# Softmax row sums of 16 heads in one matmul set, a fourth folding transfer, and seven tiles of weights in place of eight

## The chip, the cores and the metric

One core of a Trainium2 chip runs the whole program. The metric is the device time of one execution in microseconds (us). Three runs of the kernel before gave 1788.33, 1789.01 and 1789.20; the median, 1789.01, is what the changed kernel is held against.

The engines named below: PE multiplies matrices (PEld are its weight loads), ACT applies functions to elements, DVE adds and multiplies elements, POOL and SP here mostly issue DMA transfers. Each engine works through its own queue in order.

## The reference

The input is a sequence of 2048 tokens of width 1024. The output mixes two blocks with a gate per token. Block A is attention with 32 heads of width 32:

```
q, k, v = split(x @ wqkv)                      # 32 heads, width 32
scores  = q @ k.T * 32 ** -0.5
p       = softmax(scores, axis=-1)
a       = (p @ v, heads side by side) @ wo
```

Block B picks one of 64 experts for each of 32 heads per token (`peer` in the names) and sums their rows. The result is `g * a + (1 - g) * b` with `g = sigmoid((x * gate_w).sum(-1))`.

The change is in the softmax's denominators: for each head and each of the 2048 queries, the sum of `exp(score)` over all 2048 keys.

## The kernel before

The program first makes Q, K and V (Strassen-like products on PE), then runs the attention, and then multiplies by `wo`. Only the attention is touched.

Its loop runs over 512 **steps**. Step k = 16h + kt stands for key tile kt (128 keys) of head h (0 to 31). Two steps make a pair, and the order of work in a pair is written out by hand at the end of the loop: first the scores of the new pair, then the products with V of the pair before, then whatever the table `todo` holds for these steps, then the sums.

- `scores` (`L1402`) writes 128 keys x 2048 queries into four banks of `ring`, seven PSUM banks used in turn. ACT (`L1412`) takes `exp` of one, two or three banks at a time into a tile of weights: `P`, or `accd` for one key tile of each head. The cuts between these activations depend on which bank the pair begins with.
- `pv` (`L1423`) multiplies a tile of weights by V into `o`.
- `presum` adds the tiles of weights of one head to a tile of sums, `ACC[h]`. Most are added by DVE (`L1449` the first two, `L1451` the others). The key tiles in `SUMS[h]`, three or four, are kept off DVE: the first of them is written to `accd` straight away, and the others are added to it by accumulating transfers that POOL issues (`L1444`). `merge` (`L1454`) adds `accd` to `ACC[h]` on DVE, 5 steps into the next head.

**Tiles.** `P` has eight places, four in a pool on the right side of SBUF and four on the left. `p_places` gives each key tile the place that is due first, by a rule that takes a tile as read 5 steps after it was written, or 9 if a transfer reads it. An activation that writes into a place waits until its readers are through. `ACC[h]` has three tiles, taken in turn: `acc0`, `acc1` and `vhl`.

**From 128 rows to one sum.** After `merge`, `ACC[h]` holds 128 partial sums per query, one in each partition. Its upper half is added to its lower half by accumulating transfers that POOL issues: `fold_half` (`L1459`, 128 to 64 rows), `fold_quarter` (`L1462`, to 32) and, for heads 0 to 23, `fold_eighth` (`L1465`, to 16). `gather` (SP) copies the rows that are left into the tile `rb0`: eight heads of 16 rows fill its 128 partitions. Then `group_sums` (`L1435`) sums over the partitions of all these heads at once: four matmuls, one for each quarter of the queries, with a matrix of zeros and ones as weights (`sel8` for eight heads, `sel` for four). ACT copies the result to `ssb` (`L1484`), SP stores one row per head to DRAM (`smd`), `load_r` brings back the sums of four heads as 128 x 64 (`rr`), and `norm_r` (DVE `L1517`, `L1518`) makes the factors, which SP stores to `rd`.

The heads form the sets 0 to 7, 8 to 15, 16 to 23 (16 rows each) and 24 to 27 (32 rows each, without `fold_eighth`). Heads 28 to 30 go through `head_sums` with a matmul set of their own, and head 31 is done after the loop.

The due steps stand in the table `todo`. Counted from the first step of head h: `merge` 21, `fold_half` 25, `fold_quarter` 32, `fold_eighth` 39, `gather` 44, and for the last head of a set `group_sums` 52, then `load_r` 6 and `norm_r` 10 steps after that, each group of four heads 6 steps after the one before. They only set the place in each engine's queue; an instruction also waits for its data.

SP's queue in each head holds, in order: the store of the head before (`od<-osb`, key tile 0), five loads of K and Q for the next head (key tile 2), a quarter of V for the next four heads (key tile 7), a piece of `wo` (key tile 11, from head 8 on), and a `gather` (key tile 12).

Of the kernel before, what the change touches and what calls it, by code (L numbers as in the profile page):

```python
# [9 lines left out]
F32 = mybir.dt.float32  # L10
# [21 lines left out]
def gated_mha_peer_kernel(ctx, tc, xT, wqkv, wv, wo, wq, k12, ug, v, out):  # L32
# [8 lines left out]
    nc = tc.nc  # L41
# [24 lines left out]
    ident = const.tile([128, 128], F32, name="ident")  # L66
    ones = const.tile([128, 32], F32, name="ones")
# [5 lines left out]
    warm = const.tile([128, 112], F32, name="fill")  # L73
# [4 lines left out]
    def dma(dst, src, queue=nc.sync):  # L78
        a, b = (ap.bitcast(F32) if ap.dtype == F32R else ap for ap in (dst, src))
        return queue.dma_start(a, b)  # L80
# [588 lines left out]
    wl_, wh_, pools = [], [], []  # L669
# [588 lines left out]
    P, pools = {}, {}  # L1258
# [2 lines left out]

    def p_places():

        due, last, order = list(range(-8, 0)), [0] * 8, []
        for k in range(H * NT):
            h, kt = divmod(k, NT)
            if kt != SUMS[h][0]:
                i = min(range(8), key=lambda j: due[j])
                due[i], last[i] = k + (9 if kt in SUMS[h] else 5), k
                order.append(i)  # L1270
        by_last = sorted(range(8), key=lambda j: last[j])
        return iter([by_last.index(i) for i in order])

    def p_tile(h, kt):

        i = next(pools["places"])
        P[h, kt] = pools["left" if i >= 4 else "right"].tile([128, S], F32, name=f"P{i}")
        return P[h, kt]

    def first_scores(*banks):  # L1280
# [40 lines left out]
    ACC = {}  # L1321

    def new_acc(h):
        if h % 3 == 2 and h < H - 2:
            ACC[h] = keep.tile([128, S], F32, name="vhl")
        else:
            ACC[h] = wk.tile([128, S], F32, name=f"acc{h % 3 if h < H - 2 else h % 2}", bufs=1)

    def load_vhl(i):
        if i == 0:  # L1330
# [7 lines left out]
    wk = Pool("wk", bufs=2)  # L1338

    new_acc(0)  # L1340
    nc.vector.memset(sel, 0.0)
    for i in range(4):
        nc.vector.memset(sel[32 * i:32 * i + 32, i:i + 1], 1.0)
    sel8 = warm[:, :32]
    nc.vector.tensor_reduce(sel8[:, :8], ident.rearrange("p (j r) -> p j r", j=8), axis=AX.X, op=OP.max)
    nc.vector.memset(sel8[:, 8:], 0.0)
    vpool = Pool("vpool", bufs=2)
    kq = Pool("kq")
    pools["left"] = Pool("ppl")
# [79 lines left out]

    def rowsum(ps, *srcs, by=ones):
        for src in srcs:
            for qc in range(NQ):
                yield nc.tensor.matmul(ps[32 * qc:32 * qc + 32, :], by,  # L1435
                                       src[:, qc * 512:(qc + 1) * 512],
                                       start=(src is srcs[0]), stop=(src is srcs[-1]))

# [25 lines left out]
    def fold_eighth(h):  # L1464
        nc.gpsimd.dma_start(ACC[h][:16], ACC[h][16:32], accum_op=OP.add)  # L1465

    NE = 24

    def set_of(h):
        return (h // 8 * 8, 8) if h < NE else (NE, 4)  # L1470

    def gather(h):
        first, n = set_of(h)
        if h == first:
            F[first] = keep.tile([128, S], F32, name="rb0")
        rows, j = 128 // n, h - first
        dma(F[first][rows * j:rows * j + rows], ACC.pop(h)[:rows])

    def group_sums(first, n):
        i, = ring_banks(1)  # L1480
        for ins in rowsum(ring[:, i, :], F.pop(first), by=sel8 if n == 8 else sel):
            on_ring(ins, i)
        o = wk.tile([128, 512], F32, name="ssb")
        on_ring(nc.scalar.activation(o, ring[:, i, :], AF.Copy), i)  # L1484
# [80 lines left out]
    def at(step, f, *a):  # L1565
        todo.setdefault(step, []).append((f, a))

    for h in range(H):
        base = h * NT
        g, j = divmod(h, 4)  # L1570
        if h < H - 1:
            at(base + NT, finish, h)
            at(base + NT + 5, merge, h)
            if h >= NP:
                at(base + NT + 8, head_sums, h)
            else:
                at(base + NT + 9, fold_half, h)
                first, n = set_of(h)
                if n == 8:
                    at(base + 2 * NT, fold_quarter, h)  # L1580
                    at(base + 2 * NT + 7, fold_eighth, h)
                    at(base + 2 * NT + 12, gather, h)
                else:
                    at(base + 2 * NT + 4, fold_quarter, h)
                    at(base + 2 * NT + 8, gather, h)
                if h == first + n - 1:
                    step = base + (3 * NT + 4 if n == 8 else 2 * NT + 14)
                    at(step, group_sums, first, n)
                    for i in range(n // 4):
                        at(step + 6 + 6 * i, load_r, first // 4 + i)  # L1590
# [320 lines left out]
```

## Time and profile before

| what | us |
|---|---|
| three runs, median | 1789.01 (1788.33 to 1789.20) |
| the profiled execution | 1789.59 |
| its span in the trace | 1787.5 |
| PE busy (ends of matmuls modelled) | 1782.3 |
| DVE busy | 1513.2 |
| ACT busy | 1307.3 |
| POOL busy | 297.3 |

The shares change with the stage. In the page's 40 slices ACT is busy nine tenths or more in the 15th to the 36th, and one to six tenths everywhere else: that is the attention loop, from about 606 to 1611 us, and what matters here lies in it. The granted TensorE clock is full in all slices. The rows of the trace give the start in us from the span's start, the length, the engine, the line of the program, the operation, the tiles it writes and reads, and in brackets the idle time of the engine before it with what ended it ("issue" is time in which it waited for nothing that the profile shows). A group's row gives the count, the busy time, the mean of one in ns, and the idle time before them.

### The profile page before, as it was taken

The page shows a single profiled execution, that of the slowest core. Times are in us where ns is not written, and L with a number is a line of the kernel's source. Part 1 is how long each engine was busy: PE and PEld are TensorE (multiplying, and loading weights), DVE is VectorE, ACT ScalarE, POOL GpSimd, SP SyncE. Part 2 cuts the span into 40 slices and gives each one's busy share as a digit, 9 for nine tenths or more (in the row PEclk, how much of TensorE's full clock was granted, in tenths as well). Part 3 has the DMA queues.
Part 4 walks back from the last instruction along what each step waited for, and adds up shares of the span by engine and source line. Part 5 has one row for each costly group of instructions (what it writes and reads, how often), then busy time and mean ns, then how long its engine had stood idle before and what let it go on. Part 6 is the DMA issues. An engine that isn't in the chain of part 4 may idle for free.

```text
span 1787.5 us, 26063 instructions
## 1 busy us (share of the span) xinstructions
PE 1782.3 (100%) x9871; PEld 1090.3 (61%) x9871; DVE 1513.2 (85%) x1309; ACT 1307.3 (73%) x1705; POOL 297.3 (17%) x439
## 2 busy tenths in 40 slices
PE   9999999999999999999999999999999999999999
PEld 7777777888888644444444444444444444447887
DVE  8866876779997898989899998989989898887874
ACT  6545544532453699999999999999999999994221
POOL 1222222244213101111111111111111110000000
PEclk9999999999999999999999999999999999999999
DMA  8887687361348669899999999998989897888541
GB/s 286 315 310 267 223 311 294 131 210 58 113 174 293 210 142 200 173 197 183 176 206 194 199 191 203 194 189 197 191 188 195 189 196 173 198 190 300 205 160 59
DMA packets 120167, 361.17 MB, mean 202 GB/s; under 512 B 17800, under 2 KB 51864, under 8 KB 97320
## 3 DMA queue, kind: packets, MB, share of 16 engines
q0 software_dynamic: 31808, 160.76, 40.2%
q1 hardware_dynamic: 87456, 197.55, 35.6%
q8 instruction: 78, 1.28, 0.3%
q10 hardware_dynamic: 776, 1.19, 0.2%
q14 instruction: 49, 0.40, 0.1%
HBM read 173.04 MB, written 72.36 MB: 137 GB/s over the span
## 4 chain that ended last, share of the span: by engine, by line
PE 97%; DMA 1%; DVE 1%; issue 0%; ACT 0%; DVEq 0%; SPq 0%; ACTq 0%
PE ring L1402 29%; PE o L1423 26%; PE bk L304 15%; PE bk L987 7%; PE pa L987 7%; PE bk L729 5%; PE bk L292 2%; PE bk L346 2%; PE bk L1003 1%; PE pa L1662 1%; DVE acc L1451 1%; DMA wo_raw<-t0l 0%; PE bk L194 0%; DMA smd<-ssb 0%; DMA rb<-rd 0%
## 5 line engine op out<-in xcount | busy, mean ns | idle before, releaser
L1412 ACT ACTIVATE P<-ring 128x1024 f32<-128x1024 f32 (+2 forms) x1027 | 910.6, 987 | 16.7 <-PE ring L1402 0.6
L1451 DVE TENSOR_TENSOR acc<-acc,P 128x2048 f32<-128x2048 f32 x230 | 527.1, 2292 | 34.9 <-ACT P L1412 14.5
L1423 PE MATMUL o<-P,V 128*32 128x512 f32 x3840 | 464.8, 599 | 0.0
L1402 PE MATMUL ring<-Q,K 98*128 98x512 f32 x1024 | 272.3, 408 | 0.0
L1402 PEld LDWEIGHTS ring<-Q,K 98*128 98x128 f32 x1024 | 182.0, 188 | 144.6 <-ACT P L1412 80.3
L1402 PE MATMUL ring<-z,z 98*128 98x512 f32 x1016 | 269.5, 407 | 0.0
L1402 PEld LDWEIGHTS ring<-z,z 98*128 98x128 f32 x1016 | 180.8, 188 | 141.5 <-ACT P L1412 79.9
L1451 DVE TENSOR_TENSOR vhl<-vhl,P 128x2048 f32<-128x2048 f32 x104 | 238.3, 2292 | 17.7 <-ACT P L1412 8.3
L1423 PEld LDWEIGHTS o<-P,V 128*32 128x32 f32 x3840 | 98.8, 109 | 223.1 <-issue 213.7
L1444 POOL DMA_DIRECT2D accd<-P x81 | 72.1, 890 | 772.5 <-ACT P L1412 558.4
L304 PE MATMUL bk<-xh,A 128*128 128x512 f32 x336 | 81.9, 394 | 0.0
L304 PE MATMUL bk<-xh,S 128*128 128x512 f32 x336 | 81.0, 392 | 0.0
L304 PE MATMUL bk<-xl,S 128*128 128x512 f32 x336 | 79.7, 389 | 0.0
L304 PEld LDWEIGHTS bk<-xh,A 128*128 128x128 f32 x336 | 62.2, 188 | 22.0 <-issue 2.5
L139 ACT ACTIVATE hi<-u 128x512 fp32r<-128x512 f32 x42 | 26.5, 632 | 65.3 <-DVE u L520 35.6
L1449 DVE TENSOR_TENSOR acc<-P,P 128x2048 f32<-128x2048 f32 x22 | 50.4, 2292 | 26.9 <-ACT P L1412 26.8
L304 PEld LDWEIGHTS bk<-xl,S 128*128 128x128 f32 x336 | 63.0, 188 | 13.1
L304 PEld LDWEIGHTS bk<-xh,S 128*128 128x128 f32 x336 | 62.6, 188 | 12.9
L987 PE MATMUL pa<-woh,acc 128*128 128x512 f32 x216 | 70.0, 389 | 0.0
L1412 ACT ACTIVATE accd<-ring 128x1024 f32<-128x1024 f32 (+2 forms) x64 | 62.2, 1030 | 0.1
L520 DVE TENSOR_TENSOR u<-u,bk 128x512 f32<-128x512 f32 x70 | 46.6, 683 | 5.6 <-DMA wpd<-u 4.9
L1454 DVE TENSOR_TENSOR acc<-acc,accd 128x2048 f32<-128x2048 f32 x22 | 50.3, 2285 | 0.0
(329 smaller groups left out, 2323.0 us busy)
## 6 DMA issues: line engine op xcount, KB each, us to landing
accd<-P POOLq DMA_DIRECT2D x81, 1024.0 KB, 10.1
wqt<-in_wq SPq DMA_DIRECT2D x48, 512.0 KB
wraw<-in_wqkv SPq DMA_DIRECT2D x28, 512.0 KB
acc<-acc POOLq DMA_DIRECT2D x19, 512.0 KB, 12.1
kd<-hi POOLq DMA_DIRECT2D x32, 256.0 KB, 3.6
kd<-lo POOLq DMA_DIRECT2D x32, 256.0 KB, 5.6
qd<-hi POOLq DMA_DIRECT2D x32, 256.0 KB, 3.4
qd<-lo POOLq DMA_DIRECT2D x32, 256.0 KB, 3.5
```

The source lines that it names most:

```text
L292: nc.tensor.matmul(b0[w, n], AW[PLAIN[w, ki]][a][:, k, :], X[f"B{ki + 1}{n + 1}"][b][:, k, :], start=first, stop=last)
L304: nc.tensor.matmul(ps, a[i][:, k, :], b[j][:, k, :], start=(k == 0 and i == j == 0), stop=(k == HC - 1 and i == 1))
L520: nc.vector.tensor_tensor(out=out, in0=a, in1=b, op=OP.add)
L729: nc.tensor.matmul(ps, x_part(a, t // 4, kc)[:, tok], b, start=first, stop=last)
L987: nc.tensor.matmul(ps, self.a[a][i][:, k, :], self.b[b][j][k], start=(not first and k == 0 and i == j == 0), stop=(k == HC - 1 and i == 1))
L1402: on_ring(nc.tensor.matmul(ring[:, i, :], K[:98, kt * 128:(kt + 1) * 128], Q[:98, qc * 512:(qc + 1) * 512], start=True, stop=True), i)
L1412: on_ring(nc.scalar.activation(P[h, kt][:, q0 * 512:(q0 + m) * 512].rearrange("p (a m) -> p a m", a=m), ring[:, i:i + m, :], AF.Exp, scale ...
L1423: nc.tensor.matmul(O[h][32 * qc:32 * qc + 32, :], Vt[g][:, kt, 32 * j:32 * j + 32], p[:, qc * 512:(qc + 1) * 512], start=(kt == 0), stop=( ...
L1444: nc.gpsimd.dma_start(ACCD[h], P[h, kt], accum_op=OP.add)
L1449: nc.vector.tensor_add(ACC[h], P[h, 0], P[h, kt])
L1451: nc.vector.tensor_add(ACC[h], ACC[h], P[h, kt])
L1454: nc.vector.tensor_add(ACC[h], ACC[h], ACCD[h])
```

## The change

The sets become 0 to 15 (8 rows a head), 16 to 23 (16 rows) and 24 to 27 (32 rows). For heads 0 to 15 a fourth accumulating transfer, `fold_sixteenth`, brings 16 rows to 8. Their `gather` comes at step 53 and `group_sums` at step 61 after the head's first. For the other heads the steps are as before.

A head's tile of sums is now in use for longer, so there are four of them: `acc0`, `acc1`, `vhl` and `acc3`. The space for `acc3` comes from the tiles of weights, of which seven are left. Under the rule of `p_places` a place that DVE reads is written again 7 to 9 steps later with eight places and 6 to 8 with seven; a place that a transfer reads, 11 to 13 and 10 to 12 steps later. The pool on the left now holds three places and `acc3`.

The matrices of zeros and ones are made on DVE by one reduction and one fill each, in the same way for all three sets.

```
-        due, last, order = list(range(-8, 0)), [0] * 8, []
+        due, last, order = list(range(-7, 0)), [0] * 7, []
...
-        P[h, kt] = pools["left" if i >= 4 else "right"].tile([128, S], F32, name=f"P{i}")
+        P[h, kt] = pools["right" if i in (0, 1, 4, 5) else "left"].tile([128, S], F32, name=f"P{i}")
...
     def new_acc(h):
-        if h % 3 == 2 and h < H - 2:
+        i = h % 4 if h < H - 2 else 3 if h == H - 2 else 1
+        if i == 2:
             ACC[h] = keep.tile([128, S], F32, name="vhl")
+        elif i == 3:
+            ACC[h] = pools["left"].tile([128, S], F32, name="acc3")
         else:
-            ACC[h] = wk.tile([128, S], F32, name=f"acc{h % 3 if h < H - 2 else h % 2}", bufs=1)
+            ACC[h] = wk.tile([128, S], F32, name=f"acc{i}", bufs=1)
...
-    nc.vector.memset(sel, 0.0)
-    for i in range(4):
-        nc.vector.memset(sel[32 * i:32 * i + 32, i:i + 1], 1.0)
-    sel8 = warm[:, :32]
-    nc.vector.tensor_reduce(sel8[:, :8], ident.rearrange("p (j r) -> p j r", j=8), axis=AX.X, op=OP.max)
-    nc.vector.memset(sel8[:, 8:], 0.0)
+    SETS = {0: (16, [8] * 16), 16: (8, [16] * 8), 24: (4, [32] * 4)}
+    by = {0: sel, 16: warm[:, :32], 24: warm[:, 32:64]}
+    for first, (n, rows) in SETS.items():
+        nc.vector.tensor_reduce(by[first][:, :n], ident.rearrange("p (j r) -> p j r", j=n), axis=AX.X, op=OP.max)
+        nc.vector.memset(by[first][:, n:], 0.0)
...
+    def fold_sixteenth(h):
+        nc.gpsimd.dma_start(ACC[h][:8], ACC[h][8:16], accum_op=OP.add)
...
+    def rows_of(h):
+        first = set_of(h)
+        rows = SETS[first][1]
+        return sum(rows[:h - first]), rows[h - first]
...
+        first, (r0, n) = set_of(h), rows_of(h)
...
-        dma(F[first][rows * j:rows * j + rows], ACC.pop(h)[:rows])
+        dma(F[first][r0:r0 + n], ACC.pop(h)[:n])
...
-        for ins in rowsum(ring[:, i, :], F.pop(first), by=sel8 if n == 8 else sel):
+        for ins in rowsum(ring[:, i, :], F.pop(first), w=by[first]):
...
-                if n == 8:
-                    at(base + 2 * NT, fold_quarter, h)
-                    at(base + 2 * NT + 7, fold_eighth, h)
-                    at(base + 2 * NT + 12, gather, h)
-                else:
-                    at(base + 2 * NT + 4, fold_quarter, h)
-                    at(base + 2 * NT + 8, gather, h)
+                folds = {32: {36: fold_quarter}, 16: {32: fold_quarter, 39: fold_eighth},
+                         8: {32: fold_quarter, 39: fold_eighth, 46: fold_sixteenth}}[rows]
+                for step, f in folds.items():
+                    at(base + step, f, h)
+                at(base + {32: 40, 16: 44, 8: 53}[rows], gather, h)
                 if h == first + n - 1:
-                    step = base + (3 * NT + 4 if n == 8 else 2 * NT + 14)
+                    step = base + {32: 46, 16: 52, 8: 61}[rows]
```

PE's queue loses the set of heads 0 to 7 in head 10, between a pair's products with V and the next scores; the set of heads 8 to 15 moves from head 18, key tile 4, to key tile 13 and covers all sixteen. Before, in head 10:

```order
L1402 MATMUL ring_5537<-z1_4922,z0_4921 128x512 x8
L1423 MATMUL o_7638<-P3_7625,V_6452 32x512 x4
L1423 MATMUL o_7638<-P4_7633,V_6452 32x512 x4
L1435 MATMUL ring_5537<-rb0_6108,fill_96 32x512 x4
L1402 MATMUL ring_5537<-z1_4922,z0_4921 128x512 x8
```

The same place of the changed kernel (lines are a few numbers further on):

```order
L1404 MATMUL ring_5536<-z1_4922,z0_4921 128x512 x8
L1425 MATMUL o_7644<-P0_7631,V_6453 32x512 x4
L1425 MATMUL o_7644<-P6_7639,V_6453 32x512 x4
L1404 MATMUL ring_5536<-z1_4922,z0_4921 128x512 x8
L1425 MATMUL o_7644<-P3_7662,V_6453 32x512 x4
```

The row with `rb0` is gone; the products of a pair are followed at once by the next scores.

POOL's queue before, from an `accd<-P` of an odd head on (`vhl`, `acc0`, `acc1` are tiles of sums of three heads in a row):

```order
L1444 DMA accd_6980<-P1_7105 128x2048
L1462 DMA acc0_6817<-acc0_6817 32x2048
L1444 DMA accd_7189<-P7_7214 128x2048
L1465 DMA acc0_6817<-acc0_6817 16x2048
L1444 DMA accd_7189<-P0_7289 128x2048
L1459 DMA acc1_7025<-acc1_7025 64x2048
L1444 DMA accd_7189<-P2_7341 128x2048
L1462 DMA acc1_7025<-acc1_7025 32x2048
L1444 DMA accd_7398<-P0_7447 128x2048
```

The same stretch of the changed kernel (`vhl` now holds the sums of the head that `acc0` held, and `acc3` those of `acc1`):

```order
L1446 DMA accd_6983<-P5_7109 128x2048
L1470 DMA acc1_6610<-acc1_6610 8x2048
L1464 DMA vhl_6819<-vhl_6819 32x2048
L1446 DMA accd_7193<-P0_7218 128x2048
L1467 DMA vhl_6819<-vhl_6819 16x2048
L1446 DMA accd_7193<-P4_7294 128x2048
L1461 DMA acc3_7028<-acc3_7028 64x2048
L1446 DMA accd_7193<-P1_7346 128x2048
L1470 DMA vhl_6819<-vhl_6819 8x2048
L1464 DMA acc3_7028<-acc3_7028 32x2048
L1446 DMA accd_7403<-P2_7452 128x2048
```

The rows of `L1470` with 8 x 2048 are new. Each stands right behind the last `accd<-P` of a head and right ahead of the next head's `fold_quarter`.

SP's queue before, around the second set (`smd2` and `smd3` are the sums of heads 8 to 15):

```order
L80 DMA od_69<-osb_9322 128x2x256
L80 DMA K1_5535<-kd_63 32x2048
L80 DMA K1_5535<-kd_63 64x2048
L80 DMA Q1_5536<-qd_62 32x2048
L80 DMA Q1_5536<-qd_62 64x2048
L80 DMA Q1_5536<-shd_64 2x2048
L80 DMA smd2_73<-ssb_9383 4x512 x4
L80 DMA smd3_74<-ssb_9383 4x512 x4
L80 DMA V_8987<-vd1_66 128x4x128
L80 DMA rr_9469<-smd2_73 128x64
```

SP's queue of the changed kernel, around its first set, in heads 18 and 19:

```order
L80 DMA rb0_9471<-acc0_8921 16x2048
L80 DMA smd0_71<-ssb_9478 4x512 x4
L80 DMA smd1_72<-ssb_9478 4x512 x4
L80 DMA smd2_73<-ssb_9478 4x512 x4
L80 DMA smd3_74<-ssb_9478 4x512 x4
L80 DMA od_69<-osb_9546 128x2x256
L80 DMA z0_4921<-kd_63 32x2048
L80 DMA z0_4921<-kd_63 64x2048
L80 DMA z1_4922<-qd_62 32x2048
L80 DMA z1_4922<-qd_62 64x2048
L80 DMA z1_4922<-shd_64 2x2048
L80 DMA rr_9579<-smd0_71 128x64
```

Sixteen stores now stand in one piece ahead of the store of a head and the loads of K and Q, and the load of `rr` comes after those. The gathers of heads 0 to 15 now stand behind the loads of K and Q of a head and ahead of its V load; that of head 16 (the first row here) comes one step ahead of the set of heads 0 to 15, into the tile that this set reads.

More of the change, by code (lines that the diff above doesn't have):

```diff
@@ L1267, in p_places @@
             if kt != SUMS[h][0]:
-                i = min(range(8), key=lambda j: due[j])
+                i = min(range(7), key=lambda j: due[j])
                 due[i], last[i] = k + (9 if kt in SUMS[h] else 5), k
                 order.append(i)
-        by_last = sorted(range(8), key=lambda j: last[j])
+        by_last = sorted(range(7), key=lambda j: last[j])
         return iter([by_last.index(i) for i in order])
@@ L1424, in pv, with rowsum @@
                              p[:, qc * 512:(qc + 1) * 512], start=(kt == 0), stop=(kt == NT - 1))
-    def rowsum(ps, *srcs, by=ones):
+    def rowsum(ps, *srcs, w=ones):
         for src in srcs:
             for qc in range(NQ):
-                yield nc.tensor.matmul(ps[32 * qc:32 * qc + 32, :], by,
+                yield nc.tensor.matmul(ps[32 * qc:32 * qc + 32, :], w,
                                        src[:, qc * 512:(qc + 1) * 512],
@@ L1465, in fold_eighth @@
         nc.gpsimd.dma_start(ACC[h][:16], ACC[h][16:32], accum_op=OP.add)
-    NE = 24
+    def fold_sixteenth(h):
+        nc.gpsimd.dma_start(ACC[h][:8], ACC[h][8:16], accum_op=OP.add)
     def set_of(h):
-        return (h // 8 * 8, 8) if h < NE else (NE, 4)
+        return max(f for f in SETS if f <= h)
+    def rows_of(h):
+        first = set_of(h)
+        rows = SETS[first][1]
+        return sum(rows[:h - first]), rows[h - first]
     def gather(h):
-        first, n = set_of(h)
+        first, (r0, n) = set_of(h), rows_of(h)
         if h == first:
             F[first] = keep.tile([128, S], F32, name="rb0")
-        rows, j = 128 // n, h - first
-        dma(F[first][rows * j:rows * j + rows], ACC.pop(h)[:rows])
+        dma(F[first][r0:r0 + n], ACC.pop(h)[:n])
     def group_sums(first, n):
         i, = ring_banks(1)
-        for ins in rowsum(ring[:, i, :], F.pop(first), by=sel8 if n == 8 else sel):
+        for ins in rowsum(ring[:, i, :], F.pop(first), w=by[first]):
             on_ring(ins, i)
@@ L1577, in gated_mha_peer_kernel @@
                 at(base + NT + 9, fold_half, h)
-                first, n = set_of(h)
-                if n == 8:
-                    at(base + 2 * NT, fold_quarter, h)
-                    at(base + 2 * NT + 7, fold_eighth, h)
-                    at(base + 2 * NT + 12, gather, h)
-                else:
-                    at(base + 2 * NT + 4, fold_quarter, h)
-                    at(base + 2 * NT + 8, gather, h)
+                rows, first = rows_of(h)[1], set_of(h)
+                n = SETS[first][0]
+                folds = {32: {36: fold_quarter}, 16: {32: fold_quarter, 39: fold_eighth},
[3 more added lines that the diff above has]
+                at(base + {32: 40, 16: 44, 8: 53}[rows], gather, h)
                 if h == first + n - 1:
-                    step = base + (3 * NT + 4 if n == 8 else 2 * NT + 14)
+                    step = base + {32: 46, 16: 52, 8: 61}[rows]
                     at(step, group_sums, first, n)
```

## Prediction

> **What bounds the kernel now.** I read the page's parts on engines and on the chain first, then one row of stretches for the attention part (the first scores of `L1402` to the last product of `L1423`), then the order of time around one set of sums.
>
> ```profile
> PE 1782.3 (100%) x9871; PEld 1090.3 (61%) x9871; DVE 1513.2 (85%) x1309; ACT 1307.3 (73%) x1705; POOL 297.3 (17%) x439
> ...
> PE 97%; DMA 1%; DVE 1%; issue 0%; ACT 0%; DVEq 0%; SPq 0%; ACTq 0%
> ```
>
> ```profile
> 606.10:1610.80 1004.70, 1004.70 (x6195) 471.64 (x6193) 911.82 (x423) 984.16 (x1132) 137.23 (x162) 1.00 0.88 189
> ```
>
> The columns after the length are the busy time of PE, PEld, DVE, ACT and POOL, then the clock, the DMA share and GB/s. In these 1004.7 us two engines look full: PE, whose matmul ends are modelled, and ACT with 984.2 us (98%). DVE has 911.8 us (91%). So I look for the one that sets the pace: the weight loads of the scores (`L1402`) start a new pair of key tiles each time, and their starts are not modelled.
>
> ```profile
> 922.71 1.68 PEld L1402 LDWEIGHTS ring<-z,z 98*128 98x128 f32 x8 [0.84 <-ACT P L1412]
> ...
> 925.63 0.13 PEld L1423 LDWEIGHTS o<-P,V 128*32 128x32 f32 x4 [0.30 <-issue]
> 926.06 0.13 PEld L1435 LDWEIGHTS ring<-rb,fill 128*32 128x32 f32 x4 [0.30 <-issue]
> ...
> 926.49 0.13 PEld L1435 LDWEIGHTS ring<-rb,fill 128*32 128x32 f32 x4 [0.30 <-issue]
> 927.46 1.68 PEld L1402 LDWEIGHTS ring<-z,z 98*128 98x128 f32 x8 [0.84 <-issue]
> ...
> 927.60 0.60 ACT L1484 ACTIVATE ssb<-ring 128x512 f32<-128x512 f32 x1 [0.31 <-PE ring L1435]
> ...
> 931.36 1.69 PEld L1402 LDWEIGHTS ring<-z,z 98*128 98x128 f32 x8 [0.84 <-ACT P L1412]
> ```
>
> A pair without sums takes 931.36 - 927.46 = 3.90 us, so a step (one key tile of one head) takes 1.95. The pair with sums takes 927.46 - 922.71 = 4.75. The gap before the scores' loads is 0.84 us whether the releaser is "issue" or ACT, so it belongs to PE's own sequence. And the pair is longer by 0.85 us, which is what PE does more (two rounds of loads, 925.63 to 926.06 to 926.49, 0.43 each, 0.86 together) and not the 0.60 us that ACT does more. **PE sets the pace; ACT follows with 20.5 us of air in 1004.7.**
>
> **The Trainium skill** ("Perfetto Trace Analysis", Identifying the Most-Contended Engine) says that TensorE's matmul occupancy is a poor measure, that its weight-load share should be taken, and that for ScalarE occupancy counts: by that PE would be at 47% (471.64 of 1004.70) and ACT, at 98%, the engine to relieve. Here the pair with sums speaks against it: it grew by PE's amount.
>
> **What goes.** Four sets of sums in `group_sums` (heads 0, 8, 16, 24) become three (0, 16, 24). One set is four matmuls in the PE queue, all on the path: **-0.86 us**. Its copy on ACT (0.60 us and the 0.31 idle ahead of it) lies beside PE and is not counted again.
>
> **What is added on POOL.** Sixteen `fold_sixteenth`, each put into POOL's queue 7 steps after `fold_eighth` of the same head and waiting for its landing; behind it stand `fold_quarter` of the next head and the next `accd<-P`. An odd head and the even one after it:
>
> ```profile
> 1021.42 0.78 POOL L1465 DMA_DIRECT2D vhl<-vhl  x1 [0.23 <-DMA vhl<-vhl]
> ...
> 1033.40 0.90 POOL L1444 DMA_DIRECT2D accd<-P  x1 [9.04 <-ACT P L1412]
> 1038.66 0.79 POOL L1462 DMA_DIRECT2D acc<-acc  x1 [4.36 <-PE ring L1402]
> 1049.72 0.89 POOL L1444 DMA_DIRECT2D accd<-P  x1 [10.28 <-ACT P L1412]
> ```
>
> ```profile
> 1072.15 0.90 POOL L1444 DMA_DIRECT2D accd<-P  x1 [8.11 <-ACT P L1412]
> 1074.55 0.79 POOL L1462 DMA_DIRECT2D acc<-acc  x1 [1.49 <-DMA acc<-acc]
> 1082.83 0.90 POOL L1444 DMA_DIRECT2D accd<-P  x1 [7.49 <-ACT P L1412]
> ...
> 1086.07 0.81 POOL L1459 DMA_DIRECT2D vhl<-vhl  x1 [1.54 <-DVE vhl L1454]
> ```
>
> ```profile
> accd<-P POOLq DMA_DIRECT2D x81, 1024.0 KB, 10.1
> ...
> acc<-acc POOLq DMA_DIRECT2D x16, 128.0 KB, 12.5
> ```
>
> `fold_eighth` (`L1465`) issues at 1021.42 and lands 12.5 us later by the DMA rows, at 1033.9. The new issue comes after the `accd<-P` of 1033.40, at 1034.3, and is through by about 1035.1 (an estimate from the 0.78 to 0.81 us of the fold rows here), before 1038.66. In the even head its source landed long before; it goes from 1073.05 to about 1073.9, before 1074.55. So it fits into idle time that POOL has in both. Without that cover the next `fold_quarter` would issue about 1 us late, and behind it lie 10.28 and 7.49 us of idle time before the `accd<-P` that ACT releases. Cost 0.
>
> Its landing: no row shows 64 KB here. Bounds are the 10.1 us of 1 MB and the 12.5 us of 128 KB; I take 12.5, the nearest. That ends at 1046.8 and 1085.6. Bytes don't grow: each of these 16 heads gathers 64 KB less.
>
> **What moves on SP.** `gather` of heads 0 to 15 goes from key tile 12 of head h+2 to key tile 5 of head h+3: past one store of `osb` and five loads of K and Q, to a place just ahead of the V load.
>
> ```profile
> 1083.22 0.44 SPq L80 DMA_DIRECT2D z<-shd  x1
> 1083.70 0.38 SPq L80 DMA_DIRECT2D V<-vd  x1
> ```
>
> Of head 16 the gather also waits until PE has read the tile `rb0` for the set of heads 0 to 15, one step later; the stores behind it need that set anyway. In the even case SP comes there at 1083.7 and may wait until 1085.6, at most 1.9 us. Behind it stand a quarter of V, used 21 steps (41 us) later or more, a piece of Wo for the end of the loop, and the next head's store. Cost 0.
>
> Sixteen stores `smd<-ssb` now stand in one piece, ahead of the loads of head 20 and of `load_r`, and four `norm_r` follow 6 steps apart, for which DVE waits in order, with all its adds behind them.
>
> ```profile
> 1179.14 5.90 SPq L80 DMA_DIRECT2D smd<-ssb  x8
> ...
> 1203.88 0.34 SPq L80 DMA_DIRECT2D rr<-smd  x1
> 1204.27 0.87 SPq L80 DMA_DIRECT2D od<-osb  x1
> 1205.19 1.06 SPq L80 DMA_DIRECT2D z<-kd  x2
> 1206.30 1.16 SPq L80 DMA_DIRECT2D z<-qd  x2
> 1207.49 0.44 SPq L80 DMA_DIRECT2D z<-shd  x1
> ```
>
> ```profile
> 1197.33 0.54 DVE L1517 RECIPROCAL rr<-rr 128x64 f32<-128x64 f32 x1
> ...
> 1209.37 0.55 DVE L1517 RECIPROCAL rr<-rr 128x64 f32<-128x64 f32 x1
> ```
>
> Eight stores take 5.9 us, sixteen 11.8; with 3.7 for the store and the five loads that now stand between them and the load of `rr` (1204.27 to 1207.93), that load issues 15.5 us after the first store. It took at most 5.5 us (1203.88 to 1209.37, where DVE didn't wait), so it is there after at most 21.0 us; at the same distance of 10 steps DVE came 18.2 us after the first store (1179.14 to 1197.33). DVE may wait 0 to 2.8 us, once; the three `norm_r` after it come 11.7 us (6 steps) apart, the 12.04 us of 1197.33 to 1209.37, so I count no wait for them. K and Q of head 20 are needed 37 us (19 steps) later. Whether a wait of DVE costs anything is a matter of the tiles of weights.
>
> **Seven tiles of weights.** By the rule of `p_places`, a tile that DVE reads is written again 6 to 8 steps later instead of 7 to 9; one that a transfer reads, 10 to 12 instead of 11 to 13. The tightest of all the 6-step reuses, as the trace stands, is key tile 13 of head 6 over key tile 7:
>
> ```profile
> 804.13 1.02 ACT L1412 ACTIVATE P<-ring 128x1024 f32<-128x1024 f32 x1
> ```
>
> ```profile
> 809.55 2.29 DVE L1451 TENSOR_TENSOR acc<-acc,P 128x2048 f32<-128x2048 f32 x1
> ```
>
> ```profile
> 815.68 1.05 ACT L1412 ACTIVATE P<-ring 128x1024 f32<-128x1024 f32 x1
> ```
>
> Written from 804.13, added up by 809.55 + 2.29 = 811.84, needed at 815.68: **3.84 us of room**. For the transferred ones: 10 steps are 19.5 us, less 2.0 for the two activations that write the tile and 10.1 for landing, 7.4 us. So the eighth tile was cover that nobody used, and the wait of up to 2.8 us on DVE stays inside 3.84. Cost 0; if DVE falls X us behind, X - 3.84.
>
> Leaving out a set also shifts the ring by a bank, so that the activations are cut in other places; by the rule in `scores` there is one more in all, 1092 instead of 1091.
>
> ```profile
> L1412 ACT ACTIVATE P<-ring 128x1024 f32<-128x1024 f32 (+2 forms) x1027 | 910.6, 987 | 16.7 <-PE ring L1402 0.6
> ```
>
> This group's 16.7 us of idle time have no releaser but PE, so ACT waits for no tile now, and one activation more (under 1 us) lies in its air.
>
> **Four tiles of sums** give `new_acc` more distance, which nothing waits for now, so I count no gain.
>
> **Set-up on DVE.** Five small fills and one reduction become three of each.
>
> ```profile
> 607.26 0.35 DVE L1343 MEMSET sel<- 32x1 f32 x4
> 607.62 0.29 DVE L1345 TENSOR_REDUCE fill<-ident 128x8 f32<-128x128 f32 x1
> 607.86 0.08 DVE L1346 MEMSET fill<- 128x24 f32 x1
> ```
>
> Two more reductions at 0.29 and one more fill at 0.08, less 0.35: 0.3 us later for the first add. It lies inside the same room. Cost 0, bound 0.3.
>
> **The tail.** After the last head the transfers `smd`, `rr`, `rd`, `rb` hang on DVE's last sum.
>
> ```profile
> 1585.13 2.29 DVE L1449 TENSOR_TENSOR acc<-P,P 128x2048 f32<-128x2048 f32 x1 [3.86 <-ACT P L1412]
> ```
>
> From that row on DVE shows no idle time to the last merge, and that row waits for ACT, that is for PE's pace 12 steps before the end. So the tail moves with PE.
>
> **Sum.** -0.86 us. The profiled execution took 1789.59 us (span 1787.5 and 2.1 around it), which gives 1788.7; it lay 0.58 above the median of the runs shown, so from 1789.01 I come to **1788.15**. A measurement of this kernel can tell about 0.2%, 3.6 us, from no change.
>
> **Rivals.**
> ACT sets the pace: the set is worth what ACT spends on it, 0.60 for the copy or 0.91 with the idle ahead of it, so 1788.1 to 1788.4. For it speaks the 98%, against it the pair of 4.75 us. Chance 0.11. It is where that page of the Trainium skill would lead.
>
> The gain is eaten where the sums meet: DVE's wait for `rr` and the added 0.3 go beyond 3.84 by a microsecond or two, or PE waits for the gather of head 15, which now comes 8 steps before its sums behind another transfer. 1789 to 1791. Against it: 8 steps were the distance before, and PE's row at 926.06 shows no wait but 0.30 "issue". Chance 0.07.
>
> ```profile
> L1454 DVE TENSOR_TENSOR acc<-acc,accd 128x2048 f32<-128x2048 f32 x22 | 50.3, 2285 | 0.0
> ```
>
> Slower, by one mechanism: in even heads the new transfer starts right behind the last `accd<-P` (1072.15) and takes engine time from it. By the median it lands at 1082.3; the merge that needs it (this group, without idle time ahead of it) ended at about 1086.0 (POOL is released at 1086.07), so it started at 1083.7 (2285 ns each): 1.4 us of room. If that landing slips by X, DVE waits X - 1.4 in order, and with seven tiles ACT stalls once that passes 3.84, so from X = 5.2. At X = 6 it is 0.8 in each of 8 even heads, 6.4 us: 1794.6; at 7, 14.4 us: 1802.6. For it speaks the DMA share of 0.88; against it, that the new transfer has a sixteenth of the bytes and comes later in the queue. Chance 0.06.
>
> Faster by over 3.6 us needs waits that the trace doesn't show; 0.02.
>
> **Numbers.** The forecast itself has 0.74. Its own scatter is that of the three runs (1788.33 to 1789.20, 0.87). Range: below, 1788.15 - 0.87 - 0.3 for a pair's rounding, 1787.0; above, 1789.0 and the nearer half of the eaten gain, 1790.2. Slower by over 0.2%: 0.06 and a part of the eaten gain, 0.07; faster 0.02; the same 0.91.
>
> **What would show it.** Three places with 4.75 us between score loads at the group sums, not four, and none elsewhere; the other pairs still about 3.9. ACT's idle time still without DVE or DMA as releaser. POOL's new row of 16 at about 1 us each, `accd<-P` still released by ACT. DVE's wait ahead of the first of the four reciprocals under 3 us. I would be wrong if ACT waits for P tiles (the 3.84 are gone), if the merge waits for `accd`, or if pairs grow throughout.

## The result, and the profile after

| | before | after |
|---|---|---|
| runs | 5 | 5 |
| median (us) | 1789.01 | 1805.33 |
| lowest to highest (us) | 1788.33 to 1789.61 | 1804.44 to 1808.40 |
| profiled execution, its span (us) | 1789.59, 1787.5 | 1805.42, 1803.7 |

The ratio (here and below that of the means) is 1.0092, with a 95% interval of 1.0078 to 1.0106: by the medians the change costs 16.3 us. The prediction was 1788.15 in a range of 1787.0 to 1790.2, so it was wrong by 17.2 us.

The page of the changed kernel, first. Its line of engines, the shares of the chain that ended last, and the group of the activations that write the tiles of weights:

```profile
PE 1784.6 (99%) x9863; PEld 1090.7 (60%) x9863; DVE 1512.9 (84%) x1308; ACT 1306.9 (72%) x1705; POOL 310.0 (17%) x455
...
PE 96%; DMA 2%; DVE 1%; ACT 0%; issue 0%; SPq 0%; ACTq 0%; DVEq 0%
...
L1414 ACT ACTIVATE P<-ring 128x1024 f32<-128x1024 f32 (+2 forms) x1028 | 910.7, 984 | 33.8 <-DVE acc L1453 15.4
```

The last number is the one to see: ACT's idle time ahead of these activations grew from 16.7 to 33.8 us, and DVE's adds now end 15.4 of it. (The lines of code are two further down than before: scores `L1404`, `exp` `L1414`, adds `L1453`, reciprocal `L1524`.)

Where it happened is read from the starts of the scores on PE, by pairs of steps. This is the timeline of the changed kernel: start, length, engine, line, operation, number, and in brackets the idle time ahead and what ended it.

```profile
1220.57 2.11 PE L1404 MATMUL ring<-Q,K 98*128 98x512 f32 x8
1224.46 0.98 PE L1404 MATMUL ring<-Q,K 98*128 98x512 f32 x3
1239.16 2.77 PE L1404 MATMUL ring<-Q,K 98*128 98x512 f32 x5 [13.72 <-ACT P L1414]
1245.43 2.21 PE L1404 MATMUL ring<-z,z 98*128 98x512 f32 x8
```

The pair at step 318 (head 19, key tile 14) takes 1245.43 - 1224.46 = 20.97 us where such a pair takes 3.92. That is 17.05 too long; less the 0.86 of the removed set, 16.2, and 1789.01 + 16.2 = 1805.2. One pair holds the whole loss. Back along the waits, DVE and ACT in the same timeline:

```profile
1210.66 4.68 DVE L1453 TENSOR_TENSOR acc<-acc,P 128x2048 f32<-128x2048 f32 x2
1234.97 0.55 DVE L1524 RECIPROCAL rr<-rr 128x64 f32<-128x64 f32 x1 [19.63 <-DMA rr<-smd]
```

```profile
1238.08 1.94 ACT L1414 ACTIVATE P<-ring 128x1024 f32<-128x1024 f32 x2 [14.98 <-DVE acc L1453]
```

DVE comes to `norm_r(0)` at 1215.34 and waits 19.63 us for the load of `rr`, in order, with all its adds behind it. ACT runs out of tiles of weights and waits 14.98 us for an add, and PE waits for ACT. The other three reciprocals of this set show no wait. And SP, which issues what DVE waits for:

```profile
1194.02 22.35 SPq L80 DMA_DIRECT2D smd<-ssb  x16
1216.47 1.61 SPq L80 DMA_DIRECT2D od<-osb  x1
1218.18 2.14 SPq L80 DMA_DIRECT2D z<-kd  x2
1220.37 1.18 SPq L80 DMA_DIRECT2D z<-qd  x2
1221.60 1.13 SPq L80 DMA_DIRECT2D z<-shd  x1
1222.77 1.35 SPq L80 DMA_DIRECT2D rr<-smd  x1
```

The sixteen stores took 22.35 us, 1.40 each, where the eight of before took 5.90, 0.74 each. Then came the store and the five loads, and `rr` landed 12.2 us after its issue (1222.77 to 1234.97).

### The profile page after: what moved, and what is told of

The parts are those of the page before. It is cut to its first block, busy times and chain, and to the rows that moved or that the text cites. A ratio compares the mean times of both kernels' runs of the same rounds, so it can differ in the third digit from the quotient of the medians.

```text
span 1803.7 us, 26096 instructions
## 1 busy us (share of the span) xinstructions
PE 1784.6 (99%) x9863; PEld 1090.7 (60%) x9863; DVE 1512.9 (84%) x1308; ACT 1306.9 (72%) x1705; POOL 310.0 (17%) x455
## 4 chain that ended last, share of the span: by engine, by line
PE 96%; DMA 2%; DVE 1%; ACT 0%; issue 0%; SPq 0%; ACTq 0%; DVEq 0%
PE ring L1404 29%; PE o L1425 26%; PE bk L304 15%; PE bk L987 7%; PE pa L987 7%; PE bk L729 5%; PE bk L292 2%; PE bk L346 2%; PE bk L1003 1%; DMA rr<-smd 1%; PE pa L1668 1%; DVE acc L1453 1%; DMA wo_raw<-t0l 0%; PE bk L194 0%; DMA rb<-rd 0%
## 5 line engine op out<-in xcount | busy, mean ns | idle before, releaser
L1414 ACT ACTIVATE P<-ring 128x1024 f32<-128x1024 f32 (+2 forms) x1028 | 910.7, 984 | 33.8 <-DVE acc L1453 15.4
L1453 DVE TENSOR_TENSOR acc<-acc,P 128x2048 f32<-128x2048 f32 x264 | 604.9, 2291 | 35.8 <-ACT P L1414 11.9
L1404 PE MATMUL ring<-Q,K 98*128 98x512 f32 x1024 | 273.9, 409 | 13.7 <-ACT P L1414 13.7
L1404 PEld LDWEIGHTS ring<-Q,K 98*128 98x128 f32 x1024 | 182.5, 188 | 159.3 <-ACT P L1414 99.4
L1404 PE MATMUL ring<-z,z 98*128 98x512 f32 x1016 | 269.6, 407 | 0.0
L1404 PEld LDWEIGHTS ring<-z,z 98*128 98x128 f32 x1016 | 180.8, 188 | 142.5 <-ACT P L1414 75.7
L1453 DVE TENSOR_TENSOR vhl<-vhl,P 128x2048 f32<-128x2048 f32 x70 | 160.4, 2291 | 16.4 <-ACT P L1414 10.9
L1451 DVE TENSOR_TENSOR acc<-P,P 128x2048 f32<-128x2048 f32 x25 | 57.3, 2292 | 31.3 <-ACT P L1414 31.1
L1414 ACT ACTIVATE accd<-ring 128x1024 f32<-128x1024 f32 (+2 forms) x64 | 62.1, 1030 | 0.1
L1456 DVE TENSOR_TENSOR acc<-acc,accd 128x2048 f32<-128x2048 f32 x25 | 57.1, 2285 | 0.0
```

Source lines behind the costliest of these rows:

```text
L1404: on_ring(nc.tensor.matmul(ring[:, i, :], K[:98, kt * 128:(kt + 1) * 128], Q[:98, qc * 512:(qc + 1) * 512], start=True, stop=True), i)
L1414: on_ring(nc.scalar.activation(P[h, kt][:, q0 * 512:(q0 + m) * 512].rearrange("p (a m) -> p a m", a=m), ring[:, i:i + m, :], AF.Exp, scale ...
L1451: nc.vector.tensor_add(ACC[h], P[h, 0], P[h, kt])
L1453: nc.vector.tensor_add(ACC[h], ACC[h], P[h, kt])
L1456: nc.vector.tensor_add(ACC[h], ACC[h], ACCD[h])
```

## The experiments

Three theories stood against each other. A: SP is occupied too long ahead of the loads that others wait for. B: the stores, their number or their place, are slow by themselves in some way that the order does not mend. C: the seven tiles of weights, or the added transfers, cost the time. The expectations below narrow A and B to the question of each run, so that the letters mean what each of them says. The medians of before in this section were taken on the same chip as the experiment and beside it. In the code, `...` stands for lines that are left out.

### Seven tiles and four tiles of sums, but sets of 8

```
-    SETS = {0: (16, [8] * 16), 16: (8, [16] * 8), 24: (4, [32] * 4)}
+    SETS = {0: (8, [16] * 8), 8: (8, [16] * 8), 16: (8, [16] * 8), 24: (4, [32] * 4)}
...
```

> The changed kernel with its seven tiles of weights and its fourth tile for sums, but with sets of 8 heads as before the change (no fold to 8 rows, four sets of sums, 8 stores at a time). Theory A (the late rr of the 16 stores is the loss): 1789.0 as before the change, 1788.5 to 1789.6, every pair of steps 3.9 us but for the four with sums. Theory C (seven tiles cost by themselves): over 1791, with waits of ACT for tiles spread over the loop.

Measured 1788.58 (1788.02 to 1789.25, 11 runs), before 1788.53; ratio 0.9997, interval 0.9988 to 1.0006. Its eight stores on SP:

```profile
1179.01 5.91 SPq L80 DMA_DIRECT2D smd<-ssb  x8
```

The seven tiles, the fourth tile of sums and the new order of tiles cost nothing that this comparison resolves, and in the trace the pairs over 4 us stand at the same steps as before. Theory C falls for those; the fold to 8 rows is not in this kernel, but it is in the two versions further down that lose nothing.

### `norm_r` twelve steps later

```
-                        at(step + 6 + 6 * i, load_r, first // 4 + i)
-                        at(step + 10 + 6 * i, norm_r, first // 4 + i)
+                        late = n == 16
+                        at(step + 6 + (18 if late else 6) * i, load_r, first // 4 + i)
+                        at(step + (22 + 18 * i if late else 10 + 6 * i), norm_r, first // 4 + i)
```

> The changed kernel, with norm_r(0) of the set of 16 heads put 12 steps (23 us) later in DVE's order, and the three pairs of load_r and norm_r behind it spread out; the stores and the first load of rr stay where they are. DVE then comes about 4 us after rr landed (1234.95 in the changed kernel's trace). Theory A, the late rr is the whole loss: the pair of 20.97 us is back at 3.9 and the time is 1788.2 (1787.5 to 1789.5). Theory B, the burst on SP delays all that is behind it, and K and Q of head 20 are next: their last piece landed at 1234.8, and the scores of step 320 would start at 1228.4 without DVE's wait, so the pair at step 320 waits up to 6.4 us and the time is 1791 to 1795. Theory C, the seven tiles or the added transfers cost the time: it stays at 1800 or more.

Measured 1796.54 (one run), before 1788.53. DVE does not wait for `rr` any more, and half the loss stays. Here "theory B" of the expectation is right, K and Q being next. SP and PE in its timeline:

```profile
1193.62 19.09 SPq L80 DMA_DIRECT2D smd<-ssb  x16
...
1219.90 1.25 SPq L80 DMA_DIRECT2D z<-qd  x2
```

```profile
1224.06 2.14 PE L1404 MATMUL ring<-Q,K 98*128 98x512 f32 x8
...
1234.62 3.75 PE L1404 MATMUL ring<-z,z 98*128 98x512 f32 x8 [6.57 <-DMA z<-qd]
...
1240.89 2.14 PE L1404 MATMUL ring<-z,z 98*128 98x512 f32 x8
```

PE itself waits 6.57 us for Q of head 20, whose loads stand behind the stores in SP's queue. The pair at 318 takes 10.56 us and the next 6.27, together 9.0 too long; less 0.86 and on top of 1788.53 that is 1796.7. The 2.4 of the second pair, which the expectation did not have, puts the time above its 1795. So the burst made two things late, `rr` and K and Q, and in the changed kernel the larger wait covered the smaller.

### Four stores in place of sixteen

The sums of 16 heads go to one tensor in DRAM, one transfer for each quarter of the queries, with 16 partitions instead of 4. Bytes and rows are the same.

```
+    SMALL = dram.tile([16, S], F32, name="smdall")
...
+        if n == 16:
+            for q in range(NQ):
+                dma(SMALL[:, 512 * q:512 * q + 512], o[32 * q:32 * q + 16, :])
+            return
```

> The changed kernel, with the same sums of 16 heads stored by 4 transfers of 16 partitions each instead of 16 of 4 partitions; bytes and row sizes are the same, the place is the same. Theory A, the number of issues on SP is the cost: four take 2 to 6 us, the loads of K and Q and of rr go out 16 us earlier, DVE waits under 2.7 us and nothing is lost: 1788.2, the forecast. Theory B, the bytes or rows in the full DMA engines are the cost: the four take about as long as the sixteen (over 15 us), and the time stays above 1797. Theory C (tiles, added transfers): 1800 or more.

Measured 1794.19 median, but 1788.12 to 1796.23 in 11 runs; before 1788.53; ratio 1.0024, interval 1.0015 to 1.0034. SP, DVE and the pair on PE (by its weight loads):

```profile
1193.94 6.72 SPq L81 DMA_DIRECT2D smdall<-ssb  x4
...
1209.60 0.36 SPq L81 DMA_DIRECT2D rr<-smdall  x1
```

```profile
1224.63 0.55 DVE L1529 RECIPROCAL rr<-rr 128x64 f32<-128x64 f32 x1 [9.37 <-DMA rr<-smdall]
```

```profile
1224.38 0.53 PEld L1405 LDWEIGHTS ring<-Q,K 98*128 98x128 f32 x3 [0.84 <-issue]
...
1234.52 1.69 PEld L1405 LDWEIGHTS ring<-z,z 98*128 98x128 f32 x8 [1.10 <-ACT P L1415]
```

On the number of stores theory A is right, or nearly (it said 2 to 6 us): the same bytes took 6.72 us of SP and not 22.35. On the time it is not: `rr` was issued 13.2 us earlier and landed 15.0 us after its issue, so DVE still waited 9.37 us, and the pair took 10.14. The landing of `rr` is a term of its own. The runs scatter by 8 us; one trace can't show what differs between them.

### Four stores and the later `norm_r`

Both edits together, and the same kernel a second time on another chip.

> Both edits together: the 16 heads' sums stored by 4 transfers, and norm_r(0) 12 steps later. With four stores the loads of K and Q of head 20 landed at 1218.8, 9 us before step 320 needs them, and rr at 1224.6; DVE now comes at about 1238. Theory A (one long occupation of SP, of which the late rr and the late K and Q are the two results): no wait is left, every pair of steps 3.9 us, and the time is that of the forecast, one set of sums below before: 1787.7 beside 1788.53 (1787.2 to 1788.4), with the scatter of the runs back from 8 us to about 1. Theory B (something else in this stretch is late too): a wait shows at another pair, 1790 or more.

> The kernel with four stores and the later norm_r a second time, to narrow its interval: if the removed set is worth its 0.86 us, again 1787.2 to 1788.4 and 0.5 to 1.3 us below before in the same call; if the first result was chance, level with before.

Measured 1787.46 (1787.16 to 1788.36, 11 runs) beside 1788.75 of before, ratio 0.9993 (0.9984 to 1.0002); and 1787.99 (1786.82 to 1788.77, 11 runs) beside 1788.98, ratio 0.9994 (0.9985 to 1.0003). From the page, ACT's group:

```profile
L1415 ACT ACTIVATE P<-ring 128x1024 f32<-128x1024 f32 (+2 forms) x1028 | 910.6, 984 | 16.7 <-PE ring L1405 0.6
```

ACT's idle time is back at 16.7 us, every pair without sums takes about 3.9 (two near the end 4.2, as in before), and the scatter is as small as that of before. This version is 1.29 and 0.99 us below before, as the removed 0.86 would have it. Each interval still includes no change, so that the gain is there is likely by the two results together, not shown by either. In the trace the place of the removed set, in head 10, takes the 3.9 us of other pairs where it took 4.75 before.

### Sixteen stores, but four at a time

The first four at step 301, the other fours at 308, 326 and 344, with the later `norm_r`; `store(j0)` holds the loop over the stores that stood here, for four heads.

```
...
+        for j0 in range(0, n, 4):
+            if n == 16 and j0:
+                at(301 + 7 + 18 * (j0 // 4 - 1), store, j0)
+            else:
+                store(j0)
```

> The changed kernel with norm_r later as before (12 steps, and 18 apart), and its sixteen small stores kept, but only the first four at step 301; the other three fours at steps 308, 326 and 344, each ahead of its load_r. Theory A (the loss is the unbroken occupation of SP ahead of the loads of K, Q and rr in a stretch of full DMA engines): no wait is left, 1787.5 as with four large stores, scatter about 1 us. Theory B (sixteen stores cost by their number wherever they stand): K and Q of head 20 or a later load comes late, 1790 or more.

Measured 1788.10 (1787.67 to 1788.75, 11 runs) beside 1788.98 of before; ratio 0.9996 (0.9987 to 1.0005). The first four in its timeline:

```profile
1193.49 5.99 SPq L80 DMA_DIRECT2D smd<-ssb  x4
```

They take 1.50 us each, as slow as in the changed kernel, but K and Q go out behind these four and nothing is late. With the same later `norm_r` and the sixteen in one piece the time was 1796.54. So what decided was the unbroken piece ahead of other loads, not that there are sixteen.

### Fewer transfers in the same stretch

This kernel leaves out the accumulating transfers of heads 18 and 19, so the sums of these two heads lack those key tiles.

```
-            nc.gpsimd.dma_start(ACCD[h], P[h, kt], accum_op=OP.add)
+            if h not in (18, 19):
+                nc.gpsimd.dma_start(ACCD[h], P[h, kt], accum_op=OP.add)
```

> The changed kernel, with the seven transfers accd<-P of heads 18 and 19 left out (7 MB less for the DMA engines from step 288 to 319; the row sums of these two heads lack those tiles). The sixteen stores, their place and all that stands in SP's queue are the same. Theory A, the stores are slow because the DMA engines are full in this stretch: they fall from 1.4 us each to about 0.5 to 0.75 as before the change, 8 to 12 us in all, rr is there within 21 us of the first store, DVE waits under 3 us, K and Q are in time: 1788 (1787 to 1789.5). Theory B, sixteen small stores take 22 us on SP of themselves: DVE still waits 15 us or more, over 1800.

Measured 1788.65 (one run) beside 1788.75. The expectation counts seven transfers and 7 MB; the page counts 76 of `accd<-P` where that of the changed kernel counts 81, so five went, 5 MB. The stretch of the stores, first the changed kernel and then this one; the last three columns are clock, DMA share and GB/s:

```profile
1190.00:1198.00 8.00, 8.00 (x55) 3.42 (x54) 7.69 (x4) 7.62 (x10) 0.89 (x1) 1.00 1.03 187
1198.00:1206.00 8.00, 8.00 (x51) 3.83 (x50) 5.59 (x3) 8.00 (x11) 0.78 (x1) 1.00 0.93 164
```

```profile
1190.00:1198.00 8.00, 8.00 (x55) 3.39 (x54) 7.69 (x4) 7.62 (x11) 0.76 (x1) 1.00 0.47 52
1198.00:1206.00 8.00, 8.00 (x50) 3.86 (x49) 5.56 (x3) 7.98 (x12) 0.00 (x0) 1.00 0.21 62
```

And SP and DVE with fewer transfers:

```profile
1193.84 10.14 SPq L80 DMA_DIRECT2D smd<-ssb  x16
...
1207.35 0.36 SPq L80 DMA_DIRECT2D rr<-smd  x1
```

```profile
1215.08 0.55 DVE L1525 RECIPROCAL rr<-rr 128x64 f32<-128x64 f32 x1
```

The same sixteen stores at the same place, 10.14 us in place of 22.35, at a DMA share of 0.47 and 0.21 in place of 1.03 and 0.93. DVE does not wait, and the pairs over 4 us stand at the same steps as in the version with four stores and the later `norm_r`. The stores are slow because of the transfers that fill the DMA engines there. This is the run that separates the cause from the number of stores.

The changed kernel's own trace says the same, store by store: the eighth to the twelfth, from 1206.62 to 1209.42, took 0.48 to 0.71 us each at a share of 0.13 to 0.35 (stretches of 2 us), and all others 1.27 to 2.71. That the share is the whole of it is not shown: in the run with the set at step 308 and the gather behind it (below), the first six stores took 0.55 to 1.00 us at a share of about 1. Which transfers fill the engines may count too, and no run varies that.

### Only eight stores, at the place of the sixteen

The kernel with sets of 8, with only the set of heads 8 to 15 moved from step 292 to 301.

```
-                    step = base + {32: 46, 16: 52, 8: 61}[rows]
+                    step = base + {32: 46, 16: 52, 8: 61}[rows] + (9 if first == 8 else 0)
```

> The kernel with sets of 8 heads (1788.58, as before the change), with only the set of heads 8 to 15 moved from step 292 to 301, where the set of 16 stands in the changed kernel. Theory A, the place decides (a stretch with full DMA engines, ahead of K and Q): the 8 stores take 11 to 13 us there and not 5.9, rr comes 22 to 30 us after the first store, DVE waits 3 to 10 us: 1789 to 1796 and a larger scatter. Theory B, the number of stores decides: eight take 5.9 us anywhere, rr is there in time, 1788.5.

Measured 1790.14 median, 1788.02 to 1803.12 in 10 runs; before 1788.75; ratio 1.0020, interval 1.0001 to 1.0038.

```profile
1194.46 11.22 SPq L80 DMA_DIRECT2D smd<-ssb  x8
...
1209.05 0.35 SPq L80 DMA_DIRECT2D rr<-smd  x1
```

```profile
1222.55 0.55 DVE L1524 RECIPROCAL rr<-rr 128x64 f32<-128x64 f32 x1 [6.61 <-DMA rr<-smd]
```

Eight stores took 11.22 us here and 5.91 at step 292, and DVE waited 6.61 us. Two of the ten runs were at 1801.46 and 1803.12, with a mean clock of 0.997 and 0.996 as in the changed kernel (0.995 and 0.996), where the other eight show 1.0. The profiled execution took 1790.17, and its pair at 318, by the weight loads, 6.05 us:

```profile
1224.93 0.53 PEld L1404 LDWEIGHTS ring<-Q,K 98*128 98x128 f32 x3 [0.84 <-issue]
...
1230.98 1.68 PEld L1404 LDWEIGHTS ring<-z,z 98*128 98x128 f32 x8 [0.84 <-ACT P L1414]
```

So the place alone, nine steps later, brings the stall about in part. In the trace that is plain; in the time it is weak, a median 1.4 us above before and an interval that stays above no change only by the two slowest runs. Their clock makes a long stall of PE likely in them, but where they lost their time was not seen. All five runs of the changed kernel were at 1804 or more.

### The set seven steps later, twice

The first of these runs moved the set of 16 to step 308, behind the loads of K and Q, and left all else.

> The changed kernel, with the set of 16 heads 7 steps later (step 308 in place of 301, key tile 4 of a head, where the sets stood before the change): the 16 stores are then behind the loads of K and Q and not ahead of them. Theory A, the place ahead of the loads is what delays rr: the stores take 0.74 us each as they did there before, 11.8 in all, rr is there about 17 us after the first store, DVE (18.2 after it) does not wait, 1788.2. Theory B, sixteen stores are slow wherever they stand (1.4 us each, 22.4 in all): rr is there 27 us after the first, DVE waits about 9 us, and with about 2.6 us of room PE loses 6.4: 1794.6. Theory C (tiles, added transfers): 1800 or more.

Measured 1803.68 (one run), for a reason that none of the theories had:

```profile
1177.35 1.64 SPq L80 DMA_DIRECT2D wo_raw<-in_wo  x1
1209.24 0.56 SPq L80 DMA_DIRECT2D rb<-acc  x1
...
1224.30 17.59 SPq L80 DMA_DIRECT2D smd<-ssb  x16
```

SP issues nothing from 1179 to 1209: the `gather` of head 16 (due at step 300) writes the tile `rb0` that PE reads only at 308, and everything behind it stood still, K and Q of head 20 among it. The run says nothing on the stores. The second moves that gather behind the set.

```
-                at(base + {32: 40, 16: 44, 8: 53}[rows], gather, h)
+                at(base + (53 if h == 16 else {32: 40, 16: 44, 8: 53}[rows]), gather, h)
...
-                    step = base + {32: 46, 16: 52, 8: 61}[rows]
+                    step = base + {32: 46, 16: 52, 8: 68}[rows]
```

> The run with the set at step 308 once more, but with the gather of head 16 moved behind the set: there it stood ahead of the set and held SP's queue from step 300 until PE had read the tile rb0 at 308, so that run said nothing on the stores. Now the loads of K and Q of head 20 go out ahead of the stores, with nothing in front. Theory A, the order (stores ahead of K and Q) is the cost: K and Q land by 1217, rr about 20 us after the first store, 1788 to 1789. Theory B, full DMA engines (share 0.9 to 1.09 from 1190 to 1230) and sixteen issues are the cost wherever they stand in this stretch: the stores take over 18 us, rr is there 25 us or more after the first, DVE waits 7 us or more, 1792 to 1800; K and Q are in time.

Measured 1790.66 (one run) beside 1788.75.

```profile
1209.28 16.35 SPq L80 DMA_DIRECT2D smd<-ssb  x16
...
1229.47 0.50 SPq L80 DMA_DIRECT2D rr<-smd  x1
```

```profile
1232.02 0.55 DVE L1524 RECIPROCAL rr<-rr 128x64 f32<-128x64 f32 x1 [3.40 <-DMA rr<-smd]
```

The run lies between the theories. The stores were slow here too (1.02 us each), though less so than the 18 us of theory B; but `rr` landed 2.6 us after its issue and not 12.2, and DVE's 3.40 us of waiting stayed inside the room: no pair near it grew. Whether `rr` landed soon because no loads of K and Q stood just ahead of it, or because the DMA engines had room again by then, this run does not tell apart. The 2 us over before are three longer pairs from step 336 on, behind a later wait of DVE for `rr` (4.45 us) and a late load of Q of head 22.

## Why the prediction was wrong, point by point

**The step that failed** is "Eight stores take 5.9 us, sixteen 11.8; with 3.7 for the store and the five loads ... that load issues 15.5 us after the first store. It took at most 5.5 us ... so it is there after at most 21.0". The mechanism was the right one: the same queue, the same wait, the same four `norm_r`, and the prediction's own sign of being wrong (ACT waits for tiles of weights, the 3.84 us are gone) is what came. All three terms of the sum were too small:

| us | forecast | changed kernel |
|---|---|---|
| sixteen stores | 11.8 | 22.4 |
| the store and five loads | 3.7 | 6.4 |
| `rr` from issue to use | 5.5 | 12.2 |
| first store to `rr` | 21.0 | 41.0 |
| DVE comes after | 18.2 | 21.3 |
| DVE waits | 0 to 2.8 | 19.6 |

The durations were taken from rows of steps 292 and 304 and carried nine steps on. The eight stores of before, from 1179.14 to 1185.04, begin in a full stretch and run into one with room; the last columns are clock, DMA share and GB/s:

```profile
1174.00:1182.00 8.00, 8.00 (x56) 3.61 (x54) 6.56 (x4) 7.62 (x10) 1.69 (x2) 1.00 1.01 251
1182.00:1190.00 8.00, 8.00 (x52) 3.68 (x48) 7.69 (x4) 7.79 (x9) 1.75 (x2) 1.00 0.74 161
```

Nine steps later the share is 1.03 and 0.93. That the place made the price is shown: with the transfers taken out the sixteen cost 10.14, and with only eight stores in the new place they cost 11.22.

"At most 5.5 us" for the landing came from one row, and the trace of before held another that speaks against it. In its third set SP issued `rr` at 1438.43, and DVE had to wait for it, 10.9 us after the issue:

```profile
1438.43 1.34 SPq L80 DMA_DIRECT2D rr<-smd  x1
```

```profile
1449.30 0.55 DVE L1517 RECIPROCAL rr<-rr 128x64 f32<-128x64 f32 x1 [0.94 <-DMA rr<-smd]
```

With 10.9 in place of 5.5 the prediction's own sum gives 26.4 us against 18.2, a wait of 8.2 and a loss of 4.4 beyond the room of 3.84, above its range.

**A second wait was missed.** "K and Q of head 20 are needed 37 us (19 steps) later" counts from the set at step 301 and stands alone: no sum of issue and landing was set against it. In the run with the later `norm_r` Q went out by 1221.15, 27.5 us after the first store and some 20 us after step 306 where its load is due (1224.06 less six pairs of 3.9). It landed at 1234.6, 13.5 us later, and PE waited 6.57 us for it as soon as the wait for `rr` was gone.

**"If DVE falls X us behind, X - 3.84"** held. The waits were 6.61, 9.37 and 19.63 us, so the rule gives 2.8, 5.5 and 15.8; the pairs were too long by 2.1 (1230.98 - 1224.93 - 3.92), 6.2 and 17.05. The deepest stall cost 1.3 more than the rule; the slower clock after it is the likely reason, but no run takes it away by itself. With 3.40 us nothing was lost.

**One set less is 0.86 us**: the pair at step 300 is now the one with the sums, 4.75 us, and three such places remain among the group sums. ("None elsewhere" overlooked the sums of heads 28 to 30, with pairs of 4.75 to 4.78 us both before and after.) **Seven tiles** and **four tiles of sums** cost nothing, as the kernel with sets of 8 shows. **The sixteen `fold_sixteenth`** cost nothing in the two versions without stalls. From the view of that line, the issues of twelve of them (the other four write `vhl`) and the landings:

```profile
L1470 POOL DMA_DIRECT2D acc<-acc x12: 805/1048/1198, 694.5 to 1160.2; - x12
...
DMA to landing us min/median/max: 8.7/9.2/12.1
```

The forecast took about 1 us and 12.5; landings were shorter, by the median. **The later gather, the set-up and one more activation** show no wait of their own; the row of activations counts 1028 where it counted 1027. (The set-up before had six fills and not five, which changes nothing in the sum.)

**The rivals.** "The gain is eaten where the sums meet" named DVE's wait for `rr`, and gave it one or two microseconds beyond the room; it was 16. "Slower, by one mechanism" put the loss at the landing of `accd`, in every even head; merges show no wait, and the loss was in one place. "ACT sets the pace" is not what decided here, since the loss came from a stall. Of the set itself it is left open by the times: the pair in head 10 is shorter by 0.85, which is PE's 0.86 and not ACT's 0.60, but ACT's 0.91 with its idle time is as near.

## What to carry to other kernels

A burst of transfers in one in-order queue is not a number times a unit price from another place: take the price from rows at the step where it will stand, with the DMA share of that stretch beside it, look at all rows of the same form and not only at the nearest, and count what stands behind it in the queue (here `rr` and K and Q) as the things that will be late. When two results come from one burst, taking away the larger wait uncovers the smaller, so ask for each load behind it how late it may be. What mended it was to put the reader later and, with that, to break the piece up or to make it four transfers. The later reader alone was not enough (1796.54), nor were the four transfers alone (1794.19); the broken piece alone was not run.

## What the runs showed of the hardware

**An issue on SP is slow where the DMA engines are full.** In the changed kernel one store of this form took 0.48 us at its fastest, at a DMA share of 0.35 or less, and 1.27 to 2.71 where the engines were full; in the run with the set at step 308 and the gather behind it, the first six took 0.55 to 1.00 at a share of about 1. Two loads of Q, 1.2 us elsewhere, took 6.54 at a share of 0.94:

```profile
1216.28 6.54 SPq L80 DMA_DIRECT2D z<-qd  x2
```

(This is the first run with the set at step 308.) What SP waits for inside such an issue no view shows, and that stays open. The number of issues counted, not the bytes: 4 took 6.72 us (1.68 each), 16 of a quarter the size 22.35 (1.40 each). The Trainium skill ("DMA: Bandwidth & Descriptors", Rules for kernel authors) says to put many small transfers together into one; these two runs agree.

**A stalled PE comes back at half its clock.** The changed kernel around the stall, in stretches of 8 us (clock, DMA share and GB/s last):

```profile
1222.00:1230.00 8.00, 3.44 (x22) 1.11 (x21) 0.00 (x0) 1.10 (x2) 0.79 (x1) 0.91 1.02 256
1230.00:1238.00 8.00, 0.00 (x0) 0.00 (x0) 2.98 (x3) 0.00 (x0) 0.00 (x0) 0.50 0.34 77
1238.00:1246.00 8.00, 6.84 (x23) 2.41 (x24) 7.59 (x4) 5.77 (x7) 0.00 (x0) 0.52 0.33 85
1246.00:1254.00 8.00, 8.00 (x51) 3.81 (x50) 7.76 (x6) 7.84 (x9) 0.00 (x0) 1.00 0.32 87
```

After the stall the clock is at 0.50 to 0.52 for two of these stretches and full in the next. In the run with the later `norm_r` the first eight matmuls after PE's wait took 3.75 us where the same eight take 2.14, and that pair was 2.4 us too long, on top of the 6.6 us of waiting. The Trainium skill ("TensorE: Matmul & The Clock Gate", What's actually happening) says that the clock falls to half after an idle window of about 3.4 us; the 0.50 here agrees. A stall of PE of this length costs more than itself.
